# Local and coarse attention with a gated feed-forward on one core: GpSimd without value products in the opening, and other times in its list schedule

## The chip, the cores and the metric

The program runs on one core of one Trainium2 chip. A core has the engines TensorE (PE, matrix products), VectorE (DVE), ScalarE (ACT), GpSimd (POOL) and SyncE (SP, which here only issues transfers). The metric is the device time of one execution in microseconds (us); the kernel before takes 1157.02 us, the median of three runs.

## The reference

What is computed, cut to its core: for 8 batches, 8 heads, 576 positions and 64 features per head, attention over means of four neighbouring positions (the coarse part, repeated to all positions), plus attention in a band of seven neighbours (the local part); then a root-mean-square norm over the 512 features of a token and a gated feed-forward of width 1536.

```python
q_d, k_d, v_d = means of q, k, v over 4 neighbouring positions
out_d = softmax(q_d @ k_d.T / sqrt(D)) @ v_d          # 144 x 144 for each head
out_up = np.repeat(out_d, 4, axis=2)
mask = np.abs(pos[:, None] - pos[None, :]) < 4         # a band of 7 offsets
out_local = softmax(where(mask, q @ k.T / sqrt(D), -1e9)) @ v
x = (out_up + out_local) as 4608 tokens of 512
xn = x / sqrt(mean(x * x) + 1e-6) * rms_g
g = xn @ w_gate
return (g / (1 + exp(-g)) * (xn @ w_val)) @ w_out
```

## The kernel before

The tokens go through in 18 chunks of 256. For each chunk c, `Attention(c)` makes the local part: eight products of queries and keys on VectorE (`score`, L757) with their sums (`score_sum`, L761), a softmax over the seven offsets, and eight value products. A value product is divided by offsets: the first `na` of the seven are made on ACT, one activation for each offset and each of two positions (`value_scalar`, L804), the last `np` on GpSimd and those between on VectorE (both `value`, L811). The seven are then summed, in chunks 0 and 1 by products with the identity on PE (L826), from chunk 2 on by VectorE (L830). `Coarse(b, hp)` makes the coarse attention of one pair of heads of a batch: scores on PE, maximum on VectorE (L508), exponentials on ACT (L518), transposes on PE with copies on ACT (L527, L534), values on PE (L541), scaling on VectorE (L554) and a store to DRAM by an ACT transfer (`store`, L557). Chunk c loads the repeated coarse rows from there by ACT transfers (`load_up`, L839), adds them (`add_up`, L845), takes the squares, norms and transposes (L855 to L914), and `Forward(c)` then runs 12 groups f of products for gate and value (L975) and, two groups later, for the output (L1010), on PE. The half-precision remainders that these need are made by VectorE or GpSimd (L999).

The weights arrive as 36 pieces of 64-bit numbers, 24 for gate and value and 12 for the output, and are decoded on the chip: the fetch on SP (L250), a scaling on ACT (L254), the last bits on GpSimd (`last_bits`, L264), a join on VectorE (`join`, L271), the high part on ACT (L281, L283) and the remainder (`split`) on VectorE (L293, L295) or GpSimd (L291). The place of the raw numbers is free for the next fetch after the join.

The opening is ordered by a list schedule that the program works out while it is built. `Plan` holds tasks with an engine (or several with a cost each), a due time, predecessors and buffers. `run` takes again and again the task that can start first by its own clock, and among those of one engine that can start within 0.15 us of each other the one with the earliest due time; the order so found is the order of each engine's queue. A transfer's end is reckoned from `MB`, the time of one megabyte, on one common transfer clock `free["DMA"]`, plus `LAND`; a task with a `lag` counts as done that long after its end. The list holds the first eight coarse parts (for the first two batches; their sums of four come from the opening loads, `OpeningSums`, L396 to L429), attention for chunks 0 to 3, seven more coarse parts, the decoding, and the feed-forward of chunks 0 to 2. Up to 10 us after the due time of chunk 3 the order found is kept as it is; what remains is handed on in this order and may be reordered by the compiler. From chunk 3 on, the work of the next chunk is interleaved by a fixed list (`steps`), with four offsets on ACT, one on VectorE and two on GpSimd.

Of the kernel before, what the change touches and what calls it, by code (L numbers as in the profile page):

```python
# [24 lines left out]
NO = 2 * FAC - 1  # L25
# [16 lines left out]
FIRST = 3  # L42
# [5 lines left out]
NEAR = 0.15  # L48
MB = 3.1
LAND = 2.0  # L50
# [21 lines left out]
class Plan:  # L72
# [34 lines left out]
    def start(self):  # L107
        free = self.free = {e: 0.0 for e in ("PE", "ACT", "DVE", "POOL", "SP", "DMA")}
        ready = self.ready = {e: [] for e in free}
        for t in self.tasks:  # L110
            t.left = len(t.after) + len(t.with_)
            for a in (*t.after, *t.with_):
                a.next.append(t)

        for t in self.tasks:
            if not t.left:
                self.open(t)
        self.left = len(self.tasks)
# [52 lines left out]
def attn_moe_kernel(  # L171
# [263 lines left out]
    class Coarse:  # L435
# [28 lines left out]
        def plan(self, at, after=()):  # L464
# [21 lines left out]
            scaled = task("DVE", 0.42, self.scaled, at, [values, inv], allocs=[og], uses=[o, z])  # L486
            stored[b, hp] = task("ACT", 0.06, self.store, at, [scaled], uses=[og], lag=2.2)
            return self
# [96 lines left out]
    class Attention:  # L585
# [6 lines left out]
        def steps(self):  # L592
# [15 lines left out]
            def value(i):  # L608
# [5 lines left out]
                self.value(i, "DVE", self.na, NO - self.np)  # L614
                self.value(i, "POOL", NO - self.np, NO)
                self.value_sum(i)
# [23 lines left out]
        def plan(self, newton="POOL", before=()):  # L640
# [39 lines left out]
            for i, (j, par, s0) in enumerate(trio):  # L680
# [9 lines left out]
                for e, o0, o1, cost in (  # L690
                    ("DVE", self.na, NO - np_, 0.2 + 0.13 * (NO - np_ - self.na)), ("POOL", NO - np_, NO, 0.1 + 0.38 * np_),
                ):
# [20 lines left out]
            for j in range(2):  # L713
                load = task("ACT", 0.12, lambda j=j: self.load_up(j), T - 30, up_ready, allocs=[ups[j]], lag=2.5)
                add = task(
# [329 lines left out]
    def decode(n):  # L1045
# [9 lines left out]
        bits = task(  # L1055
            "POOL", 0.93, lambda: last_bits("pool"), at, [got], uses=[raw],
        )
# [8 lines left out]
        else:  # L1066
            low = ("DVE", 0.85, at), ("POOL", 1.55, at)
            whole[n] = task(low, 0, lambda e: split(e.lower()), at, [hi], uses=[w])

# [13 lines left out]
    ]  # L1083
    atts = [Attention(0, 1, 2, (ps_o, "ps_o")).plan("DVE")]
    atts.append(Attention(1, 2, 2, (ps_a, "ps_a")).plan("DVE", [h.valued for h in opening] + atts[0].turns))
    done = 2 * KT
    for i, it in enumerate(coarse[done:done + EARLY]):
        Coarse(*it).plan(due[1] + 10 + 14.0 * i, atts[1].added)
    done += EARLY
    atts += [Attention(c).plan() for c in range(2, FIRST + 1)]  # L1090
    for n in range(len(pieces)):
# [111 lines left out]
```

## Time and profile before

| | us |
|---|---|
| runs, without a profile | 1157.02, 1158.94, 1156.90 |
| median | 1157.02 |
| profiled execution | 1157.72 |
| its span, first to last instruction | 1155.9 |
| PE busy | 1083.4 (94%) |
| DVE busy | 912.5 (79%) |
| ACT busy | 621.3 (54%) |
| POOL busy | 298.5 (26%) |

All rows are from the profiled execution. Busy times are shares of the whole span and so a mean over the opening and the 15 later chunks, which have different limits; the views by stretch keep them apart. In the timeline a row gives the start in us, the duration in us, the engine (with q for its queue's own instructions), the line, the operation, what it writes and reads, how many instructions it merges, and in brackets how long the engine was idle before and what ended that.

### The profile page before, as it was taken

The numbers are of one execution on the slowest core, as the hardware profiler recorded it, in microseconds if no ns is written. First come the engines' busy times: TensorE is split into PE (matmuls) and PEld (weight loads), VectorE is DVE, ScalarE is ACT, GpSimd is POOL, SyncE is SP. The second block draws the span as 40 slices with busy tenths as digits, with TensorE's granted clock in tenths as the row PEclk, the third lists the DMA queues.
The fourth block names the chain that finished last, engine by engine and source line by source line (L and its number), as shares of the span: only waits on it lengthen the run. The fifth ranks groups of instructions, "written<-read, shape, count | busy, mean of one in ns | idle before, by whom it ended". The sixth has DMA issues, their size and how long they took to land. (4 is left out here: it accounts for less than half of the span.)

```text
span 1155.9 us, 22258 instructions
## 1 busy us (share of the span) xinstructions
PE 1083.4 (94%) x8002; PEld 989.4 (86%) x8002; DVE 912.5 (79%) x1743; ACT 621.3 (54%) x2284; POOL 298.5 (26%) x485
## 2 busy tenths in 40 slices
PE   5883899999999899999999999999999999999998
PEld 4672788888899799998988989899999999999997
DVE  5796888778888979796969696988897979796332
ACT  1564663747382838373737373747374563827222
POOL 1564553334222321312131312111112121221000
PEclk8885999999999999999999999999999999999999
DMA  9995473356634353535252525222222313120000
GB/s 253 280 296 170 101 204 96 71 116 148 132 87 116 97 104 96 117 86 114 82 118 84 113 79 114 83 67 72 62 84 55 101 46 109 52 73 20 1 19 19
DMA packets 76815, 119.59 MB, mean 103 GB/s; under 512 B 26784, under 2 KB 36256, under 8 KB 76704
## 3 DMA queue, kind: packets, MB, share of 16 engines
q1 hardware_dynamic: 47520, 97.34, 28.7%
q0 software_dynamic: 8640, 15.93, 9.2%
q10 hardware_dynamic: 20544, 4.89, 2.0%
q8 instruction: 63, 1.03, 0.4%
q14 instruction: 48, 0.39, 0.1%
HBM read 106.33 MB, written 11.80 MB: 102 GB/s over the span
## 5 line engine op out<-in xcount | busy, mean ns | idle before, releaser
L1010 PE MATMUL ps_o<-wo,hs 128*128 128x512 f32 x1296 | 359.0, 400 | 11.0 <-DVE hs L999 5.8
L975 PE MATMUL ps_h<-xh,wg 128*128 128x256 f32 x1728 | 351.5, 284 | 5.2 <-ACT xh L910 2.4
L975 PE MATMUL ps_h<-xh,wv 128*128 128x256 f32 x1728 | 340.7, 280 | 3.2 <-DVE sil L985 3.1
L975 PEld LDWEIGHTS ps_h<-xh,wg 128*128 128x128 f32 x1728 | 285.4, 191 | 15.3 <-ACT xh L910 3.1
L804 ACT ACTIVATE prod<-kv,sc 128x64 f32<-128x64 f32 x1072 | 282.6, 409 | 16.9 <-DVE sc L795 13.6
L975 PEld LDWEIGHTS ps_h<-xh,wv 128*128 128x128 f32 x1728 | 280.2, 189 | 9.5 <-DVE sil L985 5.7
L1010 PEld LDWEIGHTS ps_o<-wo,hs 128*128 128x128 f32 x1296 | 221.6, 189 | 49.6 <-DVE hs L999 9.0
L975 PE MATMUL ps_h<-xl,wg 128*128 128x256 f32 x864 | 245.7, 284 | 0.3 <-DVE xl L914 0.3
L975 PE MATMUL ps_h<-xl,wv 128*128 128x256 f32 x864 | 240.9, 279 | 0.0
L982 ACT ACTIVATE sil<-ps_h 128x256 f32<-128x256 f32 x216 | 82.5, 382 | 222.8 <-PE ps_h L975 197.1
L975 PEld LDWEIGHTS ps_h<-xl,wg 128*128 128x128 f32 x864 | 165.5, 192 | 7.0 <-issue 1.0
L811 POOL TENSOR_TENSOR prod<-sc,kv 128x256 f32<-128x256 f32 x144 | 115.7, 834 | 215.9 <-DVE x_t L830 75.5
L996 ACT ACTIVATE hs<-sil 128x256 fp32r<-128x256 f32 x216 | 89.4, 416 | 149.5 <-DVE sil L990 136.5
L975 PEld LDWEIGHTS ps_h<-xl,wv 128*128 128x128 f32 x864 | 163.2, 189 | 2.0
L985 DVE SCALAR_TENSOR_TENSOR sil<-sil,ps_h 128x256 f32<-128x256 f32 x216 | 89.5, 414 | 94.5 <-ACT sil L982 81.4
L757 DVE TENSOR_TENSOR prod<-q_t,kv 128x896 f32<-128x896 f32 x140 | 151.7, 1085 | 6.3 <-DMA q_t<-in_q_band_dram 5.3
L761 DVE TENSOR_REDUCE sc<-prod 128x14 f32<-128x896 f32 x144 | 154.4, 1076 | 0.4
L830 DVE TENSOR_REDUCE x_t<-prod 128x128 f32<-128x896 f32 x128 | 136.7, 1077 | 20.4 <-ACT prod L804 14.7
L999 DVE TENSOR_TENSOR hs<-sil,hs 128x256 fp32r<-128x256 f32 x196 | 88.2, 450 | 29.7 <-ACT hs L996 29.6
L990 DVE SCALAR_TENSOR_TENSOR sil<-sil,ps_h 128x256 f32<-128x256 f32 x216 | 89.8, 416 | 6.3 <-PE ps_h L975 4.3
L362 POOL DMA_DIRECT2D qk<-in_qk_sum_dram x36 | 32.3, 896 | 181.8 <-DMA qk<-in_qk_sum_dram 156.2
L811 DVE TENSOR_TENSOR prod<-sc,kv 128x128 f32<-128x128 f32 (+2 forms) x144 | 73.9, 543 | 1.4 <-PE ps_o L826 0.3
(118 smaller groups left out, 1001.2 us busy)
## 6 DMA issues: line engine op xcount, KB each, us to landing
kv<-in_k_pad_dram SPq DMA_DIRECT2D x72, 320.0 KB
kv<-in_v_pad_dram SPq DMA_DIRECT2D x72, 320.0 KB
qk<-in_qk_sum_dram POOLq DMA_DIRECT2D x36, 288.0 KB, 4.8
out_dram<-o_sb SPq DMA_DIRECT2D x36, 256.0 KB
q_t<-in_q_band_dram SPq DMA_DIRECT2D x70, 128.0 KB
vs<-in_v_sum_dram POOLq DMA_DIRECT2D x36, 144.0 KB, 3.5
qk<-in_qk_sum_dram SPq DMA_DIRECT2D x12, 288.0 KB
wo<-in_qk_sum_dram SPq DMA_DIRECT2D x2, 1152.0 KB
```

The lines of the kernel that those rows point to most:

```text
L757: nc.vector.tensor_tensor(out=pr, in0=bcast(q[:, s0:s0 + 2], 2, NO), in1=window(k, s0), op=ALU.mult)
L761: nc.vector.tensor_reduce(out=self.sc[:, j, par, s0:s0 + 2], in_=self.pr[i], axis=AX.X, op=ALU.add,)
L804: nc.scalar.activation(out=self.pr[i][:, o, s], in_=self.v[j, par][:, s0 + s + o], func=AF.Copy, scale=p[:, s, o:o + 1],)
L811: (nc.vector if engine == "DVE" else nc.gpsimd).tensor_tensor(out=self.pr[i][:, a:b], in0=bcast(p[:, :, a:b].rearrange("p s o -> p o s"), ...
L830: nc.vector.tensor_reduce(out=self.x[j][:, s0:s0 + 2, par], in_=pr.rearrange("p o s d -> p s d o"), axis=AX.X, op=ALU.add,)
L975: nc.tensor.matmul(out=self.p[f][:, t], lhsT=wi(f)[:, 0, k], rhs=xi[:, k], start=(n == 0), stop=(n == 3 * KT - 1),)
L982: nc.scalar.activation(out=self.sil[f], in_=self.p[f][:, 0], func=AF.Tanh, scale=0.5)
L985: nc.vector.scalar_tensor_tensor(out=self.sil[f], in0=self.sil[f], scalar=1.0, in1=self.p[f][:, 0], op0=ALU.add, op1=ALU.mult,)
L990: nc.vector.scalar_tensor_tensor(out=self.sil[f], in0=self.sil[f], scalar=0.5, in1=self.p[f][:, 1], op0=ALU.mult, op1=ALU.mult,)
L996: nc.scalar.activation(out=self.hs[f][:, 0], in_=self.sil[f], func=AF.Copy)
L999: (nc.gpsimd if engine == "POOL" else nc.vector).tensor_tensor(out=self.hs[f][:, 1], in0=self.sil[f], in1=self.hs[f][:, 0], op=ALU.subtract,)
L1010: nc.tensor.matmul(out=self.o[j], lhsT=lhs[:, cols], rhs=rhs(f)[:, 0], start=(f == 0 and i == 0), stop=(f == NF - 1 and i == 2),)
```

## The change

Five things are altered. First, the numbers of the list's transfer clock: one megabyte counts 3.6 us instead of 3.1, and the clock begins at 2.5 us instead of 0. Second, the store of a coarse part counts as done 4.0 us after it (2.2 before), the load of its rows 4.5 us after it (2.5 before). Third, value products of chunks 0 to 3: chunk 0 has 2 offsets on ACT and 5 on VectorE (before 1, 4 and 2 on GpSimd), chunk 1 has 2 and 5 (before 2, 3 and 2 on GpSimd), chunks 2 and 3 have 4 and 3 (before 4, 1 and 2 on GpSimd); the cost of VectorE's product is restated. Fourth, the last bits may be made on ACT or on GpSimd. Fifth, the splits of the output weights are made on VectorE only. Chunks 4 to 17 keep their division.

```diff
-MB = 3.1
+MB = 3.6
         free = self.free = {e: 0.0 for e in ("PE", "ACT", "DVE", "POOL", "SP", "DMA")}
+        free["DMA"] = 2.5
...
-            stored[b, hp] = task("ACT", 0.06, self.store, at, [scaled], uses=[og], lag=2.2)
+            stored[b, hp] = task("ACT", 0.06, self.store, at, [scaled], uses=[og], lag=4.0)
...
-                self.value(i, "POOL", NO - self.np, NO)
+                if self.np:
+                    self.value(i, "POOL", NO - self.np, NO)
...
-                    ("DVE", self.na, NO - np_, 0.2 + 0.13 * (NO - np_ - self.na)), ("POOL", NO - np_, NO, 0.1 + 0.38 * np_),
+                    ("DVE", self.na, NO - np_, 0.1 + 0.133 * (NO - np_ - self.na) + 0.2 * (np_ > 0)), ("POOL", NO - np_, NO, 0.1 + 0.38 * np_),
...
-                load = task("ACT", 0.12, lambda j=j: self.load_up(j), T - 30, up_ready, allocs=[ups[j]], lag=2.5)
+                load = task("ACT", 0.12, lambda j=j: self.load_up(j), T - 30, up_ready, allocs=[ups[j]], lag=4.5)
...
         bits = task(
-            "POOL", 0.93, lambda: last_bits("pool"), at, [got], uses=[raw],
+            (("ACT", 0.62, at), ("POOL", 0.93, at)), 0, lambda e: last_bits(e.lower()), at, [got], uses=[raw],
         )
...
         else:
-            low = ("DVE", 0.85, at), ("POOL", 1.55, at)
-            whole[n] = task(low, 0, lambda e: split(e.lower()), at, [hi], uses=[w])
+            whole[n] = task("DVE", 0.75, lambda: split("dve"), at, [hi], uses=[w])
...
-    atts = [Attention(0, 1, 2, (ps_o, "ps_o")).plan("DVE")]
-    atts.append(Attention(1, 2, 2, (ps_a, "ps_a")).plan("DVE", [h.valued for h in opening] + atts[0].turns))
+    atts = [Attention(0, 2, 0, (ps_o, "ps_o")).plan("DVE")]
+    atts.append(Attention(1, 2, 0, (ps_a, "ps_a")).plan("DVE", [h.valued for h in opening] + atts[0].turns))
...
-    atts += [Attention(c).plan() for c in range(2, FIRST + 1)]
+    atts += [Attention(c, 4, 0).plan() for c in range(2, FIRST + 1)]
```

## Rows read from the trace of the kernel before

**Rows 1.** Busy times by stretch, with length, instructions, granted clock and transfers.

```profile
core 0: us, PE busy (x) PEld busy (x) DVE busy (x) ACT busy (x) POOL busy (x), PEclk, DMA share, GB/s
0.00:44.00 44.00, 26.36 (x138) 20.53 (x138) 25.44 (x39) 8.56 (x28) 8.20 (x11) 0.88 0.97 248
...
44.00:90.00 46.00, 38.77 (x324) 33.01 (x324) 40.98 (x69) 31.07 (x100) 30.50 (x32) 0.85 0.90 289
90.00:111.03 21.03, 2.56 (x10) 2.07 (x10) 13.66 (x29) 9.71 (x28) 11.63 (x10) 0.50 0.62 202
111.03:192.60 81.57, 72.45 (x483) 65.57 (x483) 70.12 (x116) 47.14 (x118) 39.09 (x40) 0.92 0.54 132
192.60:256.80 64.20, 60.38 (x470) 53.21 (x469) 50.85 (x96) 35.85 (x139) 21.18 (x36) 1.00 0.43 99
256.80:321.30 64.50, 61.12 (x468) 54.79 (x467) 57.18 (x106) 36.13 (x140) 22.55 (x36) 1.00 0.59 131
```

**Rows 2.** Timeline, from the last coarse store to F0's and F1's first products.

```profile
90.33 0.30 ACTq L557 DMA_DIRECT2D up<-o_g  x1
...
94.31 2.76 ACTq L839 DMA_DIRECT2D up_t<-up  x4
...
97.17 1.21 ACT L254 ACTIVATE o_sb<-wv 128x512 f32<-128x512 f32 x2 [4.60 <-DMA up_t<-up]
...
100.09 1.29 DVE L845 TENSOR_TENSOR x_t<-ps_o,up_t 128x512 f32<-128x512 f32 x2 [5.66 <-DMA up_t<-up]
...
111.03 0.58 PE L975 MATMUL ps_h<-xh,wg 128*128 128x256 f32 x1 [0.68 <-ACT xh L910]
...
192.60 0.28 PE L975 MATMUL ps_h<-xh,wg 128*128 128x256 f32 x1
```

**Rows 3.** VectorE's waits, 0 to 193 us: total, times, longest in us.

```profile
DVE vs L429 <- DMA wg<-in_v_sum_dram: 7.4, 1, 7.4
...
DVE hs L429 <- DMA wg<-in_v_sum_dram: 2.5, 1, 2.5
```

**Rows 4.** Timeline, the last gate or value split and F0's group 8.

```profile
163.07 0.74 DVE L295 SCALAR_TENSOR_TENSOR wv<-o_sb,g_sb,wv 128x512 fp32r<-128x512 f32 x1
...
166.83 0.42 PE L975 MATMUL ps_h<-xh,wg 128*128 128x256 f32 x1
```

**Rows 5.** One line's instructions (chunks 0, 1; splits): shortest, median, longest in ns.

```profile
L811 DVE TENSOR_TENSOR prod<-sc,kv x8: 657/982/2221, 44.1 to 70.5; 128x512 f32<-128x512 f32 x8
...
L811 DVE TENSOR_TENSOR prod<-sc,kv x8: 547/864/2244, 144.0 to 175.2; 128x384 f32<-128x384 f32 x8
...
L295 DVE SCALAR_TENSOR_TENSOR wg<-o_sb,g_sb,wg x12: 737/771/1751, 52.5 to 158.6; 128x512 fp32r<-128x512 f32 x12
...
L293 DVE TENSOR_TENSOR wo<-o_sb,wo x2: 679/782/886, 161.7 to 165.9; 128x512 fp32r<-128x512 f32 x2
```

**Rows 6.** VectorE by line, 44:90, 90:192, 193:290 us: busy us, mean ns, idle before.

```profile
L811 DVE TENSOR_TENSOR prod<-sc,kv 128x512 f32<-128x512 f32 x8 | 9.0, 1137 | 0.3 <-PE ps_o L826 0.3
...
L295 DVE SCALAR_TENSOR_TENSOR wg<-o_sb,g_sb,wg 128x512 fp32r<-128x512 f32 x3 | 3.1, 1019 | 0.0
...
L295 DVE SCALAR_TENSOR_TENSOR wg<-o_sb,g_sb,wg 128x512 fp32r<-128x512 f32 x9 | 8.8, 983 | 0.0
...
L811 DVE TENSOR_TENSOR prod<-sc,kv 128x384 f32<-128x384 f32 x8 | 7.7, 966 | 0.0
...
L295 DVE SCALAR_TENSOR_TENSOR wv<-o_sb,g_sb,wv 128x512 fp32r<-128x512 f32 x9 | 6.7, 749 | 0.0
...
L811 DVE TENSOR_TENSOR prod<-sc,kv 128x128 f32<-128x128 f32 x16 | 9.4, 607 | 0.0
```

**Rows 7.** ACT by line, 44 to 90 us, the same columns.

```profile
L804 ACT ACTIVATE prod<-kv,sc 128x64 f32<-128x64 f32 x16 | 4.5, 342 | 1.1 <-PE ps_o L826 1.1
```

**Rows 8.** GpSimd by line, 44 to 193 us, the same columns.

```profile
L291 POOL TENSOR_TENSOR wo<-o_sb,wo 128x512 fp32r<-128x512 f32 x10 | 15.5, 1548 | 28.2 <-ACT wo L281 28.1
L811 POOL TENSOR_TENSOR prod<-sc,kv 128x256 f32<-128x256 f32 x16 | 14.0, 880 | 1.8 <-DVE sc L795 0.9 <-DVE sc L761 0.2 <-POOL wv L264 0.2
```

## The prediction

> **What bounds the kernel now.** I read four views, in this order. First the busy times by stretch [rows 1]: each row gives the length of a stretch and the busy time of each engine in it. I cut the stretches at the first product of the feed-forward part of chunk 0 (F0, 111.03 us) and of chunk 1 (192.60 us) [rows 2]. From 192.60 us on, PE is busy 60.38 of 64.20 us and 61.12 of 64.50 us: there PE sets the pace, and of what the other engines do less almost nothing reaches the end. Before that PE is not the bound: it works 2.56 of 21.03 us between 90 and 111 us, at a granted clock of 0.50 (the 1.2 GHz level), and 72.45 of 81.57 us in F0. So the change can gain in two places only: when F0 starts, and how long F0 takes, now 81.57 us against some 64 us for each of the next two chunks. 9.1 us of F0 are PE's own idle time.
>
> Second, the timeline around the last coarse result [rows 2]. ACT stores it at 90.33 us; the load of its repeated form (`load_up`, L839) is let go at 94.31 us, 3.98 us later; VectorE uses the loaded tile at 100.09 us, 5.78 us after the load's start. While this goes on, ACT stands idle 4.60 us and VectorE 5.66 us, because the load and the addition have been put into their queues ahead of other work that was ready.
>
> Third, VectorE's waits for transfers in the opening [rows 3]: 7.4 us and 2.5 us behind additions whose data were still on the way. Fourth, what holds F0. Its fourth to last group (f = 8) begins at 166.83 us, and the last of the 24 gate and value weights that it needs was split at 163.07 us [rows 4]. The weights are decoded by VectorE (join, split), which is busy 70.12 of 81.57 us in F0 and 40.98 of 46.00 us between 44 and 90 us [rows 1]. So F0's length is VectorE's, and idle or stretched time on VectorE ahead of 163 us is what can be won back.
>
> **The change part by part.**
>
> *Value products without GpSimd, chunks 0 and 1.* Chunk 0 takes 2 offsets on ACT and 5 on VectorE, against 1, 4 and 2 on GpSimd; chunk 1 takes 2 and 5 against 2, 3 and 2. VectorE's shortest product is 0.657 us for four offsets and 0.547 us for three [rows 5], 0.110 us for one more, so five take about 0.77 us, 6.1 us for eight. Chunk 0's eight now take 9.0 us, at a mean of 1.137 us, chunk 1's 7.7 us, at 0.966 us [rows 6], because each starts together with a GpSimd product. VectorE's gain is 2.9 + 1.6 = 4.5 us. If they stay stretched, it is a loss instead: 8 x 0.11 + 8 x 0.22 = 2.6 us. I take the gain, since the partner that starts with them is gone.
>
> *Chunks 2 and 3.* Three offsets instead of one on VectorE, with four still on ACT: 16 x 0.547 = 8.8 us against 9.4 us now [rows 6]: nothing, between 0.6 us less and 3 us more, and PE is the bound there.
>
> *ACT.* Chunk 0 adds 16 activations on ACT. The sixteen of now take 4.5 us [rows 7]; so 4.5 us more, all between 44 and 90 us, where ACT is busy 31.07 of 46.00 us [rows 1]. The cover is ACT's 14.9 us of idle time; if the new ones stand ahead of the coarse exponentials in its queue, the 4.5 us fall on the chain to the last store instead.
>
> *Splits of the output weights only on VectorE.* GpSimd made ten of the twelve, 15.5 us [rows 8]; VectorE makes one in 0.679 us at best and 0.782 us at the median [rows 5]. That adds 10 x 0.68 = 6.8 us (up to 7.8 us) to VectorE, in the stretch where it is the bound. What it takes from GpSimd is on no path.
>
> *Last bits on ACT or GpSimd.* GpSimd has 29.5 us less to do (15.5 us of splits and 14.0 us of products [rows 8]), so it will mostly be free first. I cost this at nothing, since the choice falls on the engine that starts first; each one that goes to ACT is about 0.6 us there and hides in the same idle time, or adds to the case above when that is used up.
>
> *Stretch of VectorE's other work.* The splits of the gate weights take 1.019 us and 0.983 us on average against 0.737 us at best, 12 in all: 3.1 us too much; those of the value weights in F0 only 0.749 us [rows 5, 6]. The 62 joins and splits would be stretched by 62 x 0.25 = 15.5 us if all were like the first, and hardly at all if like the second. The work taken from GpSimd is 29.5 of its 81.2 us before 192.60 us, 36% [rows 1, 8]. Bounds 0 and 5.6 us (36% of 15.5 us); I take 2.5 us, a little under the middle, as the two groups are equally many.
>
> The Trainium skill ("SBUF — State Buffer", section "SBUF: two separate sides") says that a GpSimd operation and a VectorE operation with two SBUF inputs hold their shared port pair one at a time, for the whole instruction. By it VectorE could get back up to the 29.5 us that GpSimd no longer holds. The rows agree in kind (1.137 against 0.657 us) but show some 7 us on the products and 3 us on the splits.
>
> *Times of transfers.* Between 0 and 44 us 248 GB/s arrived, between 44 and 90 us 289 GB/s [rows 1], so 4.0 and 3.5 us a MB. The list counted 3.1 us from time 0; it now counts 3.6 us from 2.5 us on, and so puts the work that waits for a transfer later in each queue. Of the second wait for the value sums the whole 2.5 us comes back; the first one of 7.4 us [rows 3] has little else ready behind it and I count nothing, between 0 and 3 us. SP's transfers keep their places by buffers coming free, no wait is added to any queue, and no instruction more is issued there.
>
> *Store and load of the coarse outputs.* 4.0 us for the store is the measured 3.98 us. 4.5 us for the load is still 1.3 us short of 5.78 us, so of VectorE's 5.66 us about 4.4 us fill with ready joins, splits and score sums. ACT gets back up to the 1.7 us of its 4.60 us that were wait for the store; the 2.76 us of issuing stay. The chain itself (store, load, addition, root, turn) is not shorter: it may be late by one VectorE instruction, about 1 us, which the same instruction returns later.
>
> *Sum.* VectorE before 192.60 us: -4.5 + 6.8 - 2.5 = -0.2 us of work, and -4.4 - 2.5 = -6.9 us of idle time: 7.1 us. At VectorE's share of F0, 70.12 / 81.57 = 0.86, that is 6.1 us of F0's end, inside PE's 9.1 us. Chunk 1 then starts at about 186.5 us, and PE carries the shift to the end. The profiled execution took 1157.72 us, its span 1155.9 us and 1.8 us around it; 1157.72 - 6.1 = 1151.6 us. It lies 0.7 us above the median of 1157.02 us, so against that median I say 1151.0 us; the likeliest case by itself runs from 1147 to 1154.5 us.
>
> **The rivals.** *The coarse chain moves too.* VectorE's 2.9 us of chunk 0 and the 2.5 us of waiting lie ahead of the last store. If the coarse steps take them, the store moves from 90.33 to about 85 us, F0 starts 5.4 us earlier and is 6.1 us shorter: 1145.5 us. For it speaks that VectorE is 89% busy there; against it that the freed time may go to any ready work, and that the last transfers come late too.
>
> *ACT becomes the bound of the coarse steps; no change.* The 4.5 us and a last-bits step or two (5.7 us) stand ahead of the last exponentials: F0 starts at about 116.7 us, and what the weights win is given back: 1157 us. It decides once ACT's idle time on that chain is below 4.5 us. Against it: 14.9 us are idle.
>
> *VectorE pays for GpSimd; slower.* If the stretch stays because the last bits and the low halves keep GpSimd as busy beside it, VectorE gets 2.6 + 7.8 = 10.4 us more and wins 6.9 us of stalls: F0's last weights come 3.5 us later, 1160.5 us. It decides where the stretched mean of the new products stays above 0.9 us. For it: VectorE is the fullest engine before 163 us.
>
> The Trainium skill ("Perfetto Trace Analysis", section "Optimizing Scalar/DVE Operations") says that for a saturated VectorE handing work to ScalarE or even GpSimd may make sense, and adds that the shared port may spoil it for GpSimd. Its first half speaks against this change and gives this last rival, its second half for it.
>
> **How the numbers follow.** Forecast 0.43, coarse chain too 0.17, no change through ACT 0.17, slower through VectorE 0.23. A difference under 0.2% (2.3 us) can't be told from none here. Faster by more: 0.43 + 0.17 = 0.60; within: 0.17; slower: 0.23. The range reaches from 1143 us, a little under the second case, to 1162 us, over the last with its one late instruction; every kept bound lies in it.
>
> **What would show it.** Right: chunk 0's VectorE products near 0.77 us, no idle time over 2 us before the addition of the loaded tile, the last gate or value weight split near 157 us, F1's first product near 186.5 us and the chunks after it as long as before. Wrong: the last coarse store later than 92 us with ACT full (second rival), the last split later than 163 us with products above 0.9 us (third), or F1 early and the later chunks longer by as much, which would mean that the list's cut into a fixed and a freely ordered part moved work into PE's stretch.

## The result, and the profile after

The changed kernel takes 1163.96 us (median of 14 runs, 1161.05 to 1175.26), the kernel before in the same measurement 1156.68 us (1151.52 to 1159.43): a ratio of 1.0078, 95% interval 1.0056 to 1.0100. It is slower, by 7 us of the medians and 9 by the ratio; I had forecast 6 us less. (The ratios are those of the measurement, made from undisturbed runs alone, without the 3722.51 us that one of e11's twelve executions took, and are not the quotients of the medians beside them: 1.0126 and 1.0147 for e10, 0.9995 and 1.0018 for e11.) The profiled execution took 1163.15 us with a span of 1161.3 us, against 1157.72 and 1155.9 us. The two spans differ by 5.4 us and not by 9: before's profile is one of its slower executions (its medians in the measurements below are 1152 to 1154 us), so some 3.6 us of the loss stand in no line shown here. Lines of the code stand one or two further down than before (L811 is L813, L295 is L296, L999 is L1001).

The busy times by stretch, after, cut at the first product of each chunk's feed-forward (columns as in [rows 1]; F0 starts at 112.03 us, F1 at 191.70, F2 at 258.10, F3 at 326.90):

```profile
44.00:90.00 46.00, 41.43 (x341) 34.61 (x339) 37.49 (x72) 36.08 (x119) 16.05 (x18) 0.83 0.80 263
90.00:112.03 22.03, 2.54 (x11) 2.08 (x11) 15.60 (x32) 10.44 (x30) 7.22 (x8) 0.50 0.77 221
112.03:191.70 79.67, 70.69 (x482) 63.75 (x483) 69.15 (x117) 50.27 (x122) 25.01 (x28) 0.95 0.56 137
191.70:258.10 66.40, 60.69 (x469) 53.34 (x468) 54.47 (x94) 36.06 (x139) 17.36 (x29) 1.00 0.39 95
258.10:326.90 68.80, 64.32 (x468) 57.88 (x467) 57.95 (x106) 35.02 (x139) 18.73 (x30) 0.96 0.56 124
326.90:386.40 59.50, 58.44 (x438) 53.67 (x436) 50.77 (x102) 37.11 (x147) 16.94 (x29) 0.99 0.43 99
```

Set them against [rows 1]. F1 starts 0.9 us earlier than before (191.70 against 192.60), not 6 us. F0 itself is 1.9 us shorter (79.67 us against 81.57), but 1.8 us of that are PE's busy time (72.45 to 70.69 us, at a granted clock of 0.92 and 0.95); PE's idle time in F0, out of which the 6.1 us were to come, is 8.98 us, against 9.12 before. Then F1's chunk takes 66.40 us against 64.20 and F2's 68.80 against 64.50: 6.5 us are lost where I had said that PE carries the shift on unchanged. In F1, 1.9 us of the 2.2 are idle time of PE (3.82 to 5.71 us); in F2, 3.2 us of the 4.3 are busy time (61.12 to 64.32 us, at a clock of 1.00 and 0.96), the rest idle. From F3 on the two agree: F3's chunk is 1.0 us shorter, and the stretch behind it, to the end, some 1 us longer.

Three of the sum's terms can be read directly. VectorE's waits, after (total, times, longest in us; the first two lines are those between 0 and 44 us, the others between 44 and 112 us):

```profile
DVE z_g L548 <- ACT a_g L519: 9.8, 1, 9.8
DVE prod L759 <- DMA q_t<-in_q_band_dram: 5.3, 1, 5.3
...
DVE o_g L555 <- PE ps_h L542: 2.9, 2, 1.8
DVE wg L296 <- ACT wg L284: 2.9, 1, 2.9
DVE o_sb L272 <- ACT o_sb L255: 1.9, 1, 1.9
DVE x_t L847 <- DMA up_t<-up: 1.6, 1, 1.6
```

The two waits for the value sums, 7.4 and 2.5 us in [rows 3], are down to 0.8 us, and the wait for the loaded tile from 5.66 us [rows 2] to 1.64. But there is a wait of 9.8 us for the coarse exponentials where there was one of 0.2 us, and 2.9 us for ACT's scaled gate weight. All waits on VectorE between 0 and 44 us add up to 19.0 us after and 18.0 before, between 44 and 112 us to 13.7 and 11.4. The idle time has changed its name and grown.

The timeline of ACT and VectorE from the last store to the addition, after, shows where the 2.9 us come from (bracket: idle time before, and what ended it):

```profile
88.84 0.30 ACTq L558 DMA_DIRECT2D up<-o_g  x1
...
93.37 3.53 ACTq L841 DMA_DIRECT2D up_t<-up  x4
96.94 0.72 ACT L284 ACTIVATE wg<-o_sb,g_sb 128x512 fp32r<-128x512 f32 x1 [6.17 <-DMA wg<-in_w_out_dram]
...
97.70 0.75 DVE L296 SCALAR_TENSOR_TENSOR wg<-o_sb,g_sb,wg 128x512 fp32r<-128x512 f32 x1 [2.87 <-ACT wg L284]
...
101.36 1.29 DVE L847 TENSOR_TENSOR x_t<-ps_o,up_t 128x512 f32<-128x512 f32 x2 [1.64 <-DMA up_t<-up]
```

The last store is 1.5 us earlier than in [rows 2], but the load's issue waits 4.53 us for it (3.98 before), takes 3.53 us (2.76), and the addition comes 7.99 us after its start (5.78), with transfers busy 0.77 of the stretch, 0.62 before. ACT stands still for 6.17 us, up to the end of that issue at 96.90 us (the bracket names another transfer), and the gate weight that VectorE needs next stands behind it in ACT's queue.

VectorE by line, after: the products from 44 to 112 us and from 112 to 192 us, then in F1's and F2's chunks (busy us, mean ns, idle before):

```profile
L813 DVE TENSOR_TENSOR prod<-sc,kv 128x640 f32<-128x640 f32 x8 | 8.0, 1009 | 1.4 <-PE ps_o L828 1.4
L813 DVE TENSOR_TENSOR prod<-sc,kv 128x640 f32<-128x640 f32 x8 | 7.9, 1000 | 0.0
L813 DVE TENSOR_TENSOR prod<-sc,kv 128x384 f32<-128x384 f32 x8 | 6.9, 883 | 0.0
L813 DVE TENSOR_TENSOR prod<-sc,kv 128x384 f32<-128x384 f32 x8 | 7.5, 962 | 0.0
```

The instructions of the output weights' split, after (shortest, median, longest ns):

```profile
L294 DVE TENSOR_TENSOR wo<-o_sb,wo x12: 656/682/732, 67.5 to 179.5; 128x512 fp32r<-128x512 f32 x12
```

The splits cost what I had said (0.682 us). The products did not: 1.0 us instead of 0.77 in chunks 0 and 1, and 0.88 and 0.96 instead of 0.547 in chunks 2 and 3. The sixteen of chunks 0 and 1 one by one (shortest, median, longest ns):

```profile
L813 DVE TENSOR_TENSOR prod<-sc,kv x16: 808/823/1369, 47.0 to 174.5; 128x640 f32<-128x640 f32 x16
```

Laid beside GpSimd's timeline they fall into two groups. Seven have none of GpSimd's arithmetic beside them and took 0.81 to 0.82 us; nine have, and took 0.81 to 1.37 us, 1.15 on average, eight of them beside the last bits (L265) and one beside a remainder (L1001). One product of each kind, and what GpSimd did beside the second:

```profile
157.42 0.81 DVE L813 TENSOR_TENSOR prod<-sc,kv 128x640 f32<-128x640 f32 x1
161.54 1.28 DVE L813 TENSOR_TENSOR prod<-sc,kv 128x640 f32<-128x640 f32 x1
...
160.08 2.06 POOL L265 TENSOR_SCALAR wo<-wo 128x512 uint32<-128x512 uint16 x2
```

What I had not thought of at all is who takes the remainders of the feed-forward (`hs`, low half; L999 before, L1001 after). The list chooses VectorE or GpSimd for each; in the changed kernel it chooses GpSimd more often. In chunks 0 to 2, the first fence before, the second after (shortest, median, longest ns):

```profile
L999 POOL TENSOR_TENSOR hs<-sil,hs x20: 725/753/1167, 126.8 to 298.4; 128x256 fp32r<-128x256 f32 x20
L999 DVE TENSOR_TENSOR hs<-sil,hs x16: 411/418/2466, 121.4 to 321.2; 128x256 fp32r<-128x256 f32 x16
```

```profile
L1001 POOL TENSOR_TENSOR hs<-sil,hs x27: 717/1001/1410, 122.4 to 319.0; 128x256 fp32r<-128x256 f32 x27
...
L1001 DVE TENSOR_TENSOR hs<-sil,hs x9: 414/418/429, 121.8 to 322.7; 128x256 fp32r<-128x256 f32 x9
```

Twenty of 36 were GpSimd's, now 27. That an emptied GpSimd gets more of them is no rule: with the value products of chunks 0 and 1 alone taken from it, the list gave it 14 (e4 below), and with the whole change but 3.5 us a MB, 21 (e12). PE's waits for GpSimd's remainders in F2's chunk, before and after (total, times, longest in us):

```profile
PE ps_o L1010 <- POOL hs L999: 2.0, 2, 1.2
...
PE ps_o L1012 <- POOL hs L1001: 4.3, 2, 2.3
```

This is what PE meets there, after. GpSimd's timeline:

```profile
297.00 0.89 POOL L363 DMA_DIRECT2D qk<-in_qk_sum_dram  x1 [3.92 <-DMA qk<-in_qk_sum_dram]
297.57 1.76 POOL L1001 TENSOR_TENSOR hs<-sil,hs 128x256 fp32r<-128x256 f32 x2
...
318.96 0.72 POOL L1001 TENSOR_TENSOR hs<-sil,hs 128x256 fp32r<-128x256 f32 x1
```

PE's timeline beside it:

```profile
298.70 1.66 PE L1012 MATMUL ps_o<-wo,hs 128*128 128x512 f32 x6 [2.27 <-POOL hs L1001]
319.74 1.67 PE L1012 MATMUL ps_o<-wo,hs 128*128 128x512 f32 x6 [2.06 <-POOL hs L1001]
```

And the busy times of the stretch behind the second wait (columns as in [rows 1]):

```profile
321.30:328.10 6.80, 6.80 (x24) 5.33 (x22) 4.06 (x10) 1.17 (x2) 0.00 (x0) 0.50 0.00 0
```

A remainder stands in GpSimd's queue behind an accumulating load that itself waits 3.92 us for the load before it; PE waits 2.27 us for it, and 2.06 us for another one behind GpSimd's Newton steps. After that second wait PE is busy without a gap but its granted clock is 0.50 (the 1.2 GHz level) for 6.8 us.

### The profile page after: what moved, and what is told of

Read it like the earlier page. It is cut to its first block, busy times and chain, and to the rows that moved or that the text cites. A ratio compares the mean times of both kernels' runs of the same rounds, so it can differ in the third digit from the quotient of the medians.

```text
span 1161.3 us, 22223 instructions
## 1 busy us (share of the span) xinstructions
PE 1088.2 (94%) x8002; PEld 992.5 (85%) x8002; DVE 913.4 (79%) x1746; ACT 629.4 (54%) x2308; POOL 257.6 (22%) x442
## 5 line engine op out<-in xcount | busy, mean ns | idle before, releaser
L1012 PE MATMUL ps_o<-wo,hs 128*128 128x512 f32 x1296 | 360.0, 400 | 11.4 <-DVE hs L1001 5.8
L806 ACT ACTIVATE prod<-kv,sc 128x64 f32<-128x64 f32 x1088 | 287.4, 408 | 14.3 <-DVE sc L797 8.2
L832 DVE TENSOR_REDUCE x_t<-prod 128x128 f32<-128x896 f32 x128 | 136.8, 1077 | 22.2 <-ACT prod L806 16.2
L813 POOL TENSOR_TENSOR prod<-sc,kv 128x256 f32<-128x256 f32 x112 | 88.3, 816 | 215.2 <-DVE x_t L832 78.0
L1001 DVE TENSOR_TENSOR hs<-sil,hs 128x256 fp32r<-128x256 f32 x189 | 79.9, 423 | 29.6 <-ACT hs L998 29.6
L813 DVE TENSOR_TENSOR prod<-sc,kv 128x128 f32<-128x128 f32 (+2 forms) x144 | 77.5, 568 | 2.6 <-PE ps_o L828 1.4
```

Source lines behind the costliest of these rows:

```text
L806: nc.scalar.activation(out=self.pr[i][:, o, s], in_=self.v[j, par][:, s0 + s + o], func=AF.Copy, scale=p[:, s, o:o + 1],)
L813: (nc.vector if engine == "DVE" else nc.gpsimd).tensor_tensor(out=self.pr[i][:, a:b], in0=bcast(p[:, :, a:b].rearrange("p s o -> p o s"), ...
L832: nc.vector.tensor_reduce(out=self.x[j][:, s0:s0 + 2, par], in_=pr.rearrange("p o s d -> p s d o"), axis=AX.X, op=ALU.add,)
L1001: (nc.gpsimd if engine == "POOL" else nc.vector).tensor_tensor(out=self.hs[f][:, 1], in0=self.sil[f], in1=self.hs[f][:, 0], op=ALU.subtract,)
L1012: nc.tensor.matmul(out=self.o[j], lhsT=lhs[:, cols], rhs=rhs(f)[:, 0], start=(f == 0 and i == 0), stop=(f == NF - 1 and i == 2),)
```

## The experiments

The theories that the expectations name: A, the strided products of chunks 2 and 3 cost; B, the list's new times cost; C, the moved work of chunks 0 and 1 costs by itself; D, the order that the list happens to write costs, whichever work is in it; E, the moved work costs, wherever; F, the remainders in GpSimd's queue cost. One fact of the code matters for all of them: the list's order is kept only up to 247 us of the list's own clock, and what comes behind that is ordered by the compiler. In the traces the cut lies at about 290 us, in F2 (the expectations say 250 us, which is the list's clock).

### The parts alone

e1: the whole change, with chunks 2 and 3 as before (`Attention(c)` for `Attention(c, 4, 0)`). 

> The whole change, but chunks 2 and 3 keep their division of before (four offsets on ACT, one on VectorE, two on GpSimd). Theory A, that the loss is VectorE's three strided offsets in chunks 2 and 3 (0.88 to 0.96 us each where one took 0.54 to 0.68 us, 16 of them, about 5 us in F1 and F2): F1 and F2 take 64 to 65 us each again, 1156 to 1158 us, no slower than before. Theory B, that the loss comes with the list's new times, whatever chunks 2 and 3 do: F2 still takes 67 us or more, 1162 to 1165 us.

 Measured: 1160.32 us against 1154.15, ratio 1.0056 (1.0033 to 1.0079), between the two theories' ranges.

e2: before, and only this:

```diff
-    atts += [Attention(c).plan() for c in range(2, FIRST + 1)]
+    atts += [Attention(c, 4, 0).plan() for c in range(2, FIRST + 1)]
```

with the change's cost of VectorE's products. 

> The kernel before with chunks 2 and 3 alone at four offsets on ACT and three on VectorE. Theory A: slower by about 5 us, 1161 to 1164 us, with F1 and F2 longer and the opening up to 192 us as before. Theory B: 1157 us, within 2 us of before, since the order of the rest is that of before.

 Measured: 1153.78 us, ratio 1.0003 (0.9976 to 1.0030). The products of 0.9 us are there and cost nothing; theory A falls, PE's work covers them as I had said.

e3: before, and only the times (MB 3.6, transfers from 2.5 us on, lags 4.0 and 4.5). 

> The kernel before with the list's times alone: 3.6 us a MB from 2.5 us on, 4.0 and 4.5 us for the coarse store and load. Theory B: slower by 5 to 8 us. Theory A: the opening's stalls on the coarse load shrink and the time is 1152 to 1157 us, no slower than before.

 Measured: 1159.91 us, ratio 1.0045 (1.0020 to 1.0070), as theory B had it.

e4: before, and only chunks 0 and 1:

```diff
-    atts = [Attention(0, 1, 2, (ps_o, "ps_o")).plan("DVE")]
-    atts.append(Attention(1, 2, 2, (ps_a, "ps_a")).plan(...))
+    atts = [Attention(0, 2, 0, (ps_o, "ps_o")).plan("DVE")]
+    atts.append(Attention(1, 2, 0, (ps_a, "ps_a")).plan(...))
```

> The kernel before with the value products of chunks 0 and 1 alone taken from GpSimd (2 offsets on ACT, 5 on VectorE). After shows 1.0 us for a product of five offsets, not the 0.77 us of the prediction; so 8.0 us for eight against 9.0 and 7.7 us before, and no gain on VectorE. Both theories: 1154 to 1160 us. The last store would move by less than 2 us; if it moves later by 4 us or more, the sixteen more activations on ACT lie on the coarse chain.

 Measured: 1160.60 us, ratio 1.0056 (1.0035 to 1.0077), just over what both theories allowed.

e6: before, and only the decoding (splits of the output weights on VectorE, last bits on ACT or GpSimd). 

> The kernel before with the decoding alone changed: splits of the output weights on VectorE, last bits on ACT or GpSimd. Theory C: VectorE gets 12 splits of 0.68 us in its fullest stretch and loses some stretch; 1154 to 1160 us. Theory D: anything within 7 us of before, either way, since the list finds another order.

 Measured: 1164.40 us, ratio 1.0095 (1.0069 to 1.0120), beyond theory C's range and beyond the 7 us of theory D.

Three parts cost 0.45 to 0.95% each, and together they cost 0.78%, not their sum of 1.96%. Costs that stayed with their part would add up; these don't, which speaks for something the parts share but does not show what.

### Orders redrawn, next to no work moved

e7 and e8 change one number of the list's model and no operation. Which engine takes a remainder or an output split is still the list's choice, and a few move with it: in e7 GpSimd makes 17 of the 36 remainders and all twelve output splits (20 and ten before), in e8 20 and eleven.

```diff
-NEAR = 0.15
+NEAR = 0.2
```

> The kernel before with the window in which the list prefers the earlier due time at 0.20 us instead of 0.15 us: no work moves between engines and no transfer time changes, but from about 50 us on the queues have another order. Theory D: the time moves by 3 us or more, either way. Theory C: within 2 us of before.

 Measured: 1172.76 us, ratio 1.0158 (1.0126 to 1.0190).

```diff
-MB = 3.1
+MB = 3.2
```

> The kernel before with 3.2 us a MB instead of 3.1 us and nothing else, a fifth of the change's step, with another order from the first sums on. Theory B, that the loss grows with the list's time of transfers: slower by 1 us. Theory D: it moves by 3 us or more, either way.

 Measured: 1158.85 us, ratio 1.0045 (1.0022 to 1.0067). A fifth of the step in MB costs as much as the whole set of measured times in e3, and a tie-breaking number alone twice what the change costs. e12 does the same to the changed kernel, 3.5 for 3.6. 

> The changed kernel with one number of the list's model a little off: 3.5 instead of 3.6 us for a MB. No work differs. Theory D: a new order, so a new time, off the changed kernel's by 0.3% or more in either direction (somewhere between 0.998 and 1.016 of before). Theory E, and the theory that the measured times as such are to blame: as the changed kernel, 1.006 to 1.010.

 Measured: 1174.44 us, ratio 1.0173 (1.0144 to 1.0202), 0.95% above the changed kernel's 1.0078 for 3% less in one number (and, by the list's choice, six remainders fewer on GpSimd and one of the last bits less on ACT). It lies over theory D's range too. Theory B falls: it isn't the times as such.

### The work changed, the order kept

In e5 the list plans as before, with before's costs and choices; only what the steps of chunks 0 and 1 issue is changed:

```diff
-            for o in range(self.na):
+            for o in range(2 if self.c < 2 else self.na):
...
         def value(self, i, engine, a, b):
+            if self.c < 2:
+                if engine == "POOL":
+                    return
+                a, b = 2, NO
```

> The kernel before with its queues in the order of before, the list's costs untouched; only the instructions handed out differ: for chunks 0 and 1 two activations and one product of five offsets on VectorE at the places of before, and no GpSimd product. Theory C, that the moved work itself costs (sixteen activations more on ACT, products of 1.0 us on VectorE): slower by 4 to 6 us as with chunks 0 and 1 alone, 1158 to 1161 us. Theory D, that each new order of the list costs or gives some us by itself, whatever work is moved: within 2 us of before.

 Measured: 1152.99 us against 1154.01, ratio 0.9998 (0.9979 to 1.0016), where the same work in its own new order (e4) had 1.0056. Laid beside before's trace, PE's queue has before's order up to 396 us in it.

e9 does so for all of the change's work: chunks 2 and 3 too (`a, b = 4, NO`), and every split on VectorE (`split("dve")`). The last bits stay on GpSimd (the changed kernel makes eight of the 36 on ACT), and so do only 20 of the remainders (27). 

> The kernel before, its list with its own times, choices and order; only the instructions that the steps of chunks 0 to 3 issue are those of the change: in chunks 0 and 1 two products on ScalarE and five on VectorE, in chunks 2 and 3 four and three, none on GpSimd, and every split of the output weights on VectorE. The queues are those of before up to about 250 us (behind that the framework orders the rest itself). Theory D (the order that the list happens to write is what costs, not the work): 0.996 to 1.003 of before, about 1156 us, with the first chunk's feed-forward at 107 to 111 us. Theory E (the moved work itself costs, since VectorE's strided products of chunks 2 and 3 take 0.9 us for three offsets): 1.004 to 1.008 here too. My forecast's sum, if it were right on the work: 0.995.

 Measured: 1155.78 us against 1153.84, ratio 1.0018 (0.9995 to 1.0041). PE's order is before's up to 292 us. Theory E's least, 1.004, is at the upper end of the interval; the changed kernel's 1.0056 to 1.0100 lies wholly above it.

e11 takes from it only the splits. 

> Before with its own order; only the splits of the output weights, ten of them on GpSimd before, all on VectorE. Theory D: 0.996 to 1.003, against the 1.0095 that the same edit gave when the list was allowed to write a new order for it. Theory E: 1.004 or more, the ten splits of 0.68 us stand on VectorE.

 Measured: 1155.87 us, ratio 0.9995 (0.9969 to 1.0020), where the decoding in its own order (e6) had 1.0095, with the last bits besides.

### The order changed, the work kept

e10 is the other half: the changed kernel's list, but each step issues the work of before, as nearly as its list allows.

```diff
         def value(self, i, engine, a, b):
+            if self.c <= FIRST and b == NO and engine == "DVE":
+                self.value(i, "POOL", 5, NO)
+                a, b = 1 if self.c < 2 else 4, 5
...
-            whole[n] = task("DVE", 0.75, lambda: split("dve"), at, [hi], uses=[w])
+            whole[n] = task("DVE", 0.75, lambda: split("pool"), at, [hi], uses=[w])
```

and the products on ACT and the last bits as before. 

> The reverse: the list of the changed kernel, with its times, choices and order, but each step issues the work of before (GpSimd takes two products again, its instruction put beside VectorE's own; the output weights' splits and the last bits go to GpSimd). Theory D: slower than before by 0.4 to 1.2%, as the changed kernel, since the order is the changed one's up to about 250 us. Theory E: 0.997 to 1.003, since the work is that of before.

 Measured: 1170.80 us against 1153.84, ratio 1.0126 (1.0099 to 1.0153), a little over theory D's range. The order of the changed kernel with the work of before is slower than the changed kernel. It is not wholly before's work: the list's choices stay, so GpSimd makes all twelve output splits and 27 remainders (ten and 20 before) and is busy 141.5 us up to F3, against 133.2. So the four corners are:

| | work of before | work of the change |
|---|---|---|
| order of before | 1 | 1.0018 (0.9995 to 1.0041) |
| order of the change | 1.0126 (1.0099 to 1.0153) | 1.0078 (1.0056 to 1.0100) |

For the moved products and splits theory E falls: in before's order they cost nothing that can be told, and the same ones in the new order come with 1.0078. D is what is left: the new order goes with 0.6% more for the change's work and 1.3% more for what is nearly before's. That the work gains about 0.5% in the new order stays open (the two intervals touch, the two kernels did not run side by side, and e10 loads GpSimd more than before did). Every order here is also held against one that was there first. How that one was come by is not on record; had it been picked among several, redrawn ones would be slower for that reason alone.

### Is it GpSimd's queue?

The trace showed 4.3 us of PE's waits for GpSimd's remainders in F2 (2.0 before) and 6.8 us at half clock behind them. e13 takes them all to VectorE, in the changed list's order up to the cut (288 us); e14 does so in before, e15 in e5:

```diff
-                    ... lambda e, f=f: self.low(f, e), soon, [high], uses=[sil, hs],
+                    ... lambda e, f=f: self.low(f, "DVE"), soon, [high], uses=[sil, hs],
```

> The changed kernel; the 27 remainders (hs low halves) that GpSimd takes in chunks 0 to 2 go to VectorE at their place in the list. Theory F (GpSimd's queue is where the changed order loses): the waits of 0.4 and 4.3 us and half of the 6.8 us at half clock go, 5 to 8 us: 1156 to 1159, 1.000 to 1.004 of before. Theory D alone (any redrawn order, the place of the loss is chance): the order behind 250 us is rewritten once more, and the time falls anywhere from 1.004 to 1.016; a wait goes here and another comes there.

 Measured: 1158.75 us against 1152.29, ratio 1.0058 (1.0036 to 1.0080). 

> The kernel before with the same edit: its 20 remainders on GpSimd in chunks 0 to 2 go to VectorE. Theory F: TensorE's waits on them (2.6, 0.5 and 2.0 us) go: 1149 to 1152 where before has 1154 to 1157, 0.995 to 0.998. Theory D alone: 1.002 to 1.012, as other new orders.

 Measured: 1159.69 us, ratio 1.0069 (1.0044 to 1.0095). 

> The kernel before in its own order, chunks 0 and 1 with the change's work (two products on ScalarE, five on VectorE), and the remainders of chunks 0 to 2 on VectorE. Theory F: 0.993 to 0.998, about 1149. Theory D alone: 1.002 to 1.012.

 Measured: 1155.96 us, ratio 1.0042 (1.0015 to 1.0069). All three lie in theory D's ranges and outside theory F's.

Busy times by stretch of e13, F0, F1 and F2:

```profile
112.38:193.37 80.99, 72.90 (x483) 66.46 (x483) 67.91 (x126) 50.36 (x122) 16.23 (x18) 0.90 0.53 134
193.37:263.74 70.37, 64.38 (x470) 56.95 (x468) 57.17 (x106) 36.24 (x139) 8.47 (x18) 0.95 0.38 90
263.74:326.09 62.35, 61.43 (x469) 55.54 (x468) 57.87 (x108) 35.01 (x139) 15.52 (x24) 1.00 0.62 136
...
251.80:258.60 6.80, 6.80 (x42) 6.80 (x41) 4.68 (x9) 1.59 (x3) 1.85 (x6) 0.50 0.31 57
```

Where the wait stood, it is gone: F2's chunk takes 62.35 us instead of 68.80, 6.5 us less, inside the 5 to 8 us that theory F had promised. But F1's takes 70.37 instead of 66.40 and F0's 1.3 us more, and that is PE's busy time (64.38 against 60.69 us in F1, 72.90 against 70.69 in F0) at a lower granted clock (0.95 against 1.00, 0.90 against 0.95); PE's idle time in F1 is 5.99 us against 5.71. 6.8 us at half clock, from 251.8 us on, have come instead of those in F2, and this time not behind a long wait. PE's last two waits before it:

```profile
249.07 1.46 PE L528 MATMUL ps_a<-ident_sb,a_g 72*72 72x72 f32 x8 [0.37 <-ACT a_g L519]
250.87 0.39 PE L977 MATMUL ps_h<-xh,wv 128*128 128x256 f32 x1 [0.34 <-DVE sil L987]
```

Of 6.5 us the profiles keep 3.6 (a span of 1157.7 against 1161.3 us), the ratios some 0.2%, less than their intervals. F0 and F1 lie ahead of the cut: there PE's order is the changed kernel's (up to 288 us), so the moved work is what differs there, besides the execution (each profile is one). In before the same edit makes F2's chunk 2.7 us shorter (61.82 against 64.50 us) and the five chunks behind it, which the compiler orders anew, 5.5 us longer (297.17 against 291.65 us). That these five are where e14 loses is not shown: e11's take as long (297.73 us) at a ratio of 0.9995. Theory F is right on the place and wrong on the worth: the wait was real, and when it was taken away other losses came. And e14 (1.0069) and e15 (1.0042, against 0.9998 without the remainders in e5) qualify theory D: the list's order was kept up to 292 us, and moving remainders alone came with 0.4 to 0.7%, be it by the work or by the part that the compiler orders.

### What a bad order costs, and where

From the busy times by stretch of each kernel, in us: F0's start, the three chunks from F0 to F3, PE's idle time in them (length less busy time), their granted clock, and the five chunks from F3 to F8.

| kernel | ratio | F0 at | F0 to F3 | PE idle | clock | F3 to F8 |
|---|---|---|---|---|---|---|
| before | 1 | 111.0 | 210.2 | 16.3 | 0.97 | 291.7 |
| e11, splits in before's order | 0.9995 | 106.3 | 207.5 | 16.9 | 0.99 | 297.7 |
| e5, work of chunks 0, 1 in before's order | 0.9998 | 107.0 | 204.7 | 12.1 | 0.98 | 293.6 |
| e2, chunks 2, 3 alone | 1.0003 | 108.9 | 212.1 | 15.0 | 0.95 | 291.1 |
| e9, all work in before's order | 1.0018 | 108.7 | 208.9 | 18.2 | 0.99 | 292.6 |
| e15, e5 with remainders on VectorE | 1.0042 | 108.9 | 207.6 | 14.8 | 0.97 | 294.1 |
| e3, times alone | 1.0045 | 111.2 | 210.9 | 18.5 | 0.98 | 290.5 |
| e8, MB 3.2 | 1.0045 | 107.7 | 218.2 | 22.2 | 0.94 | 287.7 |
| e4, chunks 0, 1 alone | 1.0056 | 109.5 | 212.7 | 20.2 | 0.97 | 290.9 |
| e1, all but chunks 2, 3 | 1.0056 | 113.6 | 216.5 | 18.2 | 0.96 | 285.5 |
| e13, after with remainders on VectorE | 1.0058 | 112.4 | 213.7 | 15.0 | 0.95 | 289.5 |
| e14, before with remainders on VectorE | 1.0069 | 110.1 | 208.1 | 15.6 | 0.97 | 297.2 |
| after | 1.0078 | 112.0 | 214.9 | 19.2 | 0.97 | 291.5 |
| e6, decoding alone | 1.0095 | 106.5 | 217.8 | 21.6 | 0.94 | 297.4 |
| e10, order of after, work of before | 1.0126 | 111.5 | 219.9 | 20.3 | 0.94 | 293.1 |
| e7, NEAR | 1.0158 | 109.7 | 230.7 | 22.6 | 0.92 | 290.6 |
| e12, after with MB 3.5 | 1.0173 | 111.0 | 229.0 | 28.7 | 0.91 | 291.0 |

F0's start, on which my forecast's sum turned, doesn't go with the result (106.5 us in e6, which is 0.95% slower). The three chunks behind it do where the loss is large: the five slowest kernels have 214.9 us and more there (as have e1 and e8), with PE's idle time of 19 to 29 us (12 to 18 in before and the three kernels in before's order) and, but for the changed kernel itself, a clock of 0.94 to 0.91. e7 is the plainest, since it moves next to no work; its F0, F1 and F2:

```profile
109.70:196.26 86.56, 73.14 (x483) 67.06 (x484) 68.54 (x116) 48.11 (x119) 40.95 (x43) 0.91 0.53 135
196.26:267.47 71.21, 67.42 (x469) 59.79 (x468) 50.02 (x96) 36.48 (x139) 19.05 (x32) 0.90 0.35 83
267.47:340.39 72.92, 67.55 (x499) 60.65 (x498) 60.59 (x120) 38.95 (x156) 25.36 (x41) 0.95 0.55 124
```

F1 has as many products as in [rows 1] (469 against 470) and 3.8 us of idle time, as before; it is 7.0 us longer by PE's busy time alone, 67.42 against 60.38 us, at a clock of 0.90 instead of 1.00. F2 has 31 products more than before (499 against 468; a coarse part fell into it) and 5.4 us idle. So a slow order shows in two ways: waits in PE's queue, and slower products where the clock falls to the 1.2 GHz level. Other work falling into a stretch lengthens it too, but is no loss by itself (e7's chunks F3 to F8 have 32 products fewer, 2126 against 2158). The clock weighs most in e7: 0.90 over F1's 71.21 us means some 14 us at the lower level (twice the missing share of the clock), and the chunk is half of that longer. By the same estimate the table's three chunks hold 37 us at the lower level in e7 and 41 in e12, 13 in before and 4 in e9; of e7's 20.5 us over before some 12 are then the clock, and 6.3 are idle time. What pulls the clock down is not settled: in the changed kernel it fell behind waits of 2 us, in e13 behind waits under 0.4 us and a run of small products.

One profile is one execution, and before's own runs go from 1147 to 1161 us over all measurements; e2's queues are before's up to 190 us, and yet its F0 starts 2.1 us earlier in its profile. So the middle of the table can't be read row by row (e4's and e3's profiles are as long as before's, their medians are not); differences of 10 us and more can.

## Why the prediction was wrong, point by point

**What bounds the kernel.** Right in kind: VectorE is full in the opening, PE from F1 on. Two steps of the sum failed. The first is "that is 6.1 us of F0's end, inside PE's 9.1 us": VectorE got no idle time back (see the stalls), PE's idle time in F0 stayed at 8.98 us, and F0's end did not follow the last gate or value split, by which I had tied it to VectorE: that split ended 4.7 us later and F1 began 0.9 us earlier. The second is the last one, "PE carries the shift to the end": I took PE's pace from F1 on as given, which holds only for the queues as they stood, and F1's and F2's chunks took 2.2 and 4.3 us more. Of the 11.5 us between my -6.1 and the profiles' +5.4, the first step makes 5.2 us and the second 6.5. I named the second myself under what would be wrong, as a cut between fixed and free part that moves work into PE's stretch, and gave it no chance and no price. What the runs show in its place is the order: e7 has 1.6% for a redrawn one, e12 1.0% more than the changed kernel; in every one of the nine kernels in which the list planned anew (e1 to e4, e6 to e8, e12 and the change) the ratio was 1.0003 to 1.0173, and in none below 1 (e2's can't be told from 1, and PE's order in it is before's up to 241 us). The three that kept before's order and its choices of engine for the remainders (e5, e9, e11) lay at 0.9995 to 1.0018.

**Products in chunks 0 and 1: -4.5 us, came out at -0.8.** The shortest product of five offsets took 0.808 us, near my 0.77; the mean was 1.005 us, 16.1 us for the sixteen instead of 12.3. I took the GpSimd product that starts with them to be the cause of the stretch, and counted the stretch as gone with it. The seven that had none of GpSimd's arithmetic beside them did come out at 0.81 to 0.82 us; the other nine met the last bits and a remainder instead (1.15 us on average). So the price was right and its condition was not met: another instruction of GpSimd took the partner's place, as my third rival had it. How many meet one is a matter of the order: in e5, with GpSimd busy 77.1 us ahead of F1 instead of 55.4, the same sixteen take 14.0 us (mean 0.882).

**Products in chunks 2 and 3: 14.4 us instead of 8.8**, and even above my bound of 3 us more than before's 9.4. The term is mis-sized because I took the price from chunk 1, whose products are laid out with 64 neighbouring elements (0.547 us); those of chunks 2 and 3 are written with a stride of seven elements, and their shortest is 0.839 us (no run changes the layout alone). It cost nothing, as e2 shows (1.0003): that PE covers it was right.

**Splits of the output weights: +6.8 us, came out at +6.7.** Right, and e11 shows that they cost nothing in before's order (0.9995).

**Stretch of the gate and value splits: -2.5 us, came out at -1.9** (from 21.6 to 19.7 us for the 24). The joins, which the term took in too, got nothing back (26.5 and 26.7 us). The 36% in it is 33%: the 81.2 us leave out GpSimd's first 44 us, 89.4 us with them. The Trainium skill ("SBUF — State Buffer", section "SBUF: two separate sides") has GpSimd and VectorE hold their shared ports by turns. The trace agrees in kind and not in size: GpSimd's busy time ahead of F1 fell from 89.4 to 55.4 us, 34 us, and VectorE's products and splits got back 0.8 and 1.9 us.

**Stalls: -6.9 us, came out above zero.** This is the step that failed first. Each wait that I had priced did shrink (7.4 and 2.5 us to 0.8, 5.66 to 1.64), and VectorE's waits up to 112 us still rose from 29.4 to 32.7 us. I had priced a wait as if the ready work behind it were waiting in store; but work put in front of it is then lacking later, and the next wait in the queue takes the name (in the opening, 9.8 us for the coarse exponentials). That reading is argued from the lists of waits; no run tests it. The load behind the last store became slower too (7.99 us for 5.78), so the chain to F0, which I had left as it was, came out 1.0 us later.

**Remainders: not in my sum.** The list sent GpSimd seven more. That took 4.5 us from VectorE ahead of F1 (5.3 us for six, then 0.85 us for two), which is more than the whole fall of VectorE's busy time there (150.2 to 146.6 us); it did not reach F1's start, since PE's idle time in F0 stayed as it was. In F2 PE waited 4.3 us for GpSimd's remainders instead of 2.0. A planner's free choices are part of what a change adds, and I had read `low`'s two options in the list without asking what they would do.

**The marks I had set.** Last gate or value split near 157 us: it ended at 168.5 us (163.8 before). F1 at 186.5: 191.7. No idle time over 2 us before the addition: 1.64, right. The condition of the third rival, products above 0.9 us and the last split later than 163 us, was met, and its 1160.5 us is the nearest to the 1164 measured; and the stretch came as it said, beside last bits and remainders. But its mechanism did not make the loss: VectorE's work ahead of F1 did not grow, F1 was not late, and the same products and splits cost nothing in e9. That its number is near is luck. The first rival's earlier store came true in part (88.84 us, not 85) and was spent on the slower load. The second one's ACT did not bind: it was busy 36.08 of 46.00 us.

**What stays open.** Why a given order is good is not settled beyond the two ways above; in e13 curing the largest single wait moved the loss. Last bits on ACT were not tested in before's order, and the changed choice of engine for the remainders neither. Whether the change's work gains 0.5% in its own order was not measured side by side. No kernel here was faster than before by more than the measurement can tell.

## What to carry to other kernels

Where a planner writes the queues, a change to any of its costs is a change of the whole order; before pricing the work, find out what an order is worth by redrawing it with next to nothing moved (here 0.45 to 1.6%), and test the work inside the old order. A stall that is filled with ready work may be paid for later in the same queue, unless that work was surplus; follow the next two waits, not one. Ask of every engine that is emptied what the planner will put there, and who waits for that. And before a gain on one engine is carried to the end, name the idle time of the bounding engine that it is to come out of, and look there first afterwards: here it was 9.1 us before and 9.0 after.

## What the runs showed of the hardware that I had not expected

A VectorE product of 384 elements per partition took 0.547 us at its shortest when written side by side (chunk 1, before) and 0.839 us when written with a stride of seven elements (chunks 2 and 3, after). VectorE products of 640 elements took 0.81 to 0.82 us with none of GpSimd's arithmetic beside them (seven) and 1.15 us on average with it (nine), though GpSimd worked on other tiles. A load issued behind the store of the data that it reads took 7.99 us until its user started with transfers busy 0.77 of the time, 5.78 us at 0.62. TensorE's granted clock fell to 0.50 for 6.8 us after two waits, of 2.27 us up to 298.70 us and of 2.06 us up to 319.74 us; in e13 it fell for as long after waits of 0.37 and 0.34 us with eight 72-row products between them; and in e7 a chunk with no more idle time than before ran at 0.90 instead of 1.00.
